# Start-up work moved between queues and engines, one weight step in halves, and idle products in other places: a fused Mamba-2 scan and gated feed-forward kernel

## The chip, the cores and the metric

The kernel runs on one core of a Trainium2 chip. The time is device microseconds (us) of one execution. The kernel before took 350.05, 351.15 and 351.86 us in three runs; the median is 351.15 us. The profile is of a further execution, which took 353.19 us and whose span, from the first to the last instruction, is 351.4 us.

Engines are named as the profile names them. PE is the matrix engine TensorE, and PEld its weight loads; DVE is VectorE, ACT is ScalarE, POOL is GpSimd, and SP is the engine whose queue issues most DMAs. A "q" after a name (SPq, ACTq) means that the engine's sequencer issues a DMA or waits.

## The reference

Inputs are x (4, 8, 768, 32), a (4, 8, 768), B and C (4, 8, 768, 16), and the weights w_in (256 x 2048) and w_out (2048 x 256). The weights are double precision in DRAM. The computation, cut to what matters:

```python
# per batch and head, in chunks of 32 steps
cum = np.cumsum(np.log(np.clip(a, 1e-6, 1.0)), axis=-1)      # within a chunk
L = np.exp(cum[..., :, None] - cum[..., None, :]) * causal   # decay from step j to step i
y = ((C @ B.T) * L) @ x + (C @ state) * np.exp(cum)
state = np.exp(cum[..., -1:]) * state + sum_j(B_j x_j * np.exp(cum[..., -1:] - cum_j))
# then tokens x 256 -> 2048 -> 256
X = y.transpose(0, 2, 1, 3).reshape(3072, 256)
h = X @ w_in
out = (h / (1 + np.exp(-1.702 * h))) @ w_out
```

## The kernel before, in words

**Tokens and groups.** The 3072 tokens form six groups of 512. A group is two pairs of 128-token chunks, and the scan works on chunks of 64 tokens. For each group the scan gives `yT`, 256 features by 512 tokens. `hidden(g, f)` multiplies it by block f of `w_in` (16 blocks of 128 hidden features, two products of 512 columns each, line 881) and applies the gate on ACT (line 885). `project_all` multiplies the gated blocks by `w_out` (line 979). Group 0, and the first four blocks of group 1, go this plain way. The rest uses a scheme with seven products in place of eight (lines 937, 947, 1042 and 1049), fed with sums and differences of weight blocks that DVE makes (`mix_in`, `mix_w`).

**Weights.** They arrive as 64-bit words and are made into 32-bit floats on the chip, in ten pieces (`PIECES`). The first four pieces are two blocks of `w_in` each, pieces 4 and 5 four blocks each, and the last four pieces are `w_out`. For each piece, `fetch` issues two DMAs from SP; `fields` (lines 192 and 195) takes exponent and mantissa bits on DVE; `clamp` (lines 203 and 204) forms the power of two on ACT; `rounded` (line 208) adds the low word on DVE; `join` (lines 219 and 225) sets the sign and multiplies on DVE. `narrow(i)` runs `rounded(i)`, `fields(i + 1)` and `join(i)` in this order. Piece 4 is blocks eight to eleven. All of it runs next to the products of group 0, which wait for `w_in` block by block.

**The start.** The first four chunks are worked in log space. `az0` (rows of a) comes in by four small DMAs, two on SP and two on ACT. DVE clips it (line 338), ACT takes the logarithm (line 340), and a DVE scan gives `cum` (line 342). PE writes a causal mask (line 545) and then the differences of `cum` (`differ`, line 551) into PSUM; ACT exponentiates them into L (line 572). `load_first` brings C by four DMAs from ACT and B by four from SP, and DVE transposes both (line 612). POOL multiplies the transposed C by a head mask (`mask_first`, line 645). PE then forms the scores (line 677), the state increments (line 708) and the outputs (lines 825 and 813). DVE applies L to the scores in `weigh` (line 688). Directly behind `weigh(0)` stands `fetch(1, held=True)`, whose one-element `memset` on DVE (line 171) holds SP until then; pieces 1 to 5 and the rest of a are issued behind it on SP.

**Selectors.** POOL builds small 0/1 tables by `memset` and `affine_select`: `pick0`, the identity, the causal mask `below`, `same` (a 128 x 256 table of which one column in 32 is read), `pick`, and `whose` (64 x 384), in this order and ahead of `mask_first`. `whose` is used by products at lines 509 and 498, `pick` on ACT at line 363.

**Idle products.** `keep_busy(5, 0)` runs five products of ones with 192 columns at the start (line 437), `pads(n, t)` is n products of 32 x 32, and `dense(2)` is two more of 256 columns (line 1153). Their results are not used. In `hidden` for group 1, some of the products are cut into two or four by columns, by a count in lines 876 to 878: the first three into four and the next five into two.

**The order.** Each engine runs its instructions in the order in which they are written; `in_order` at the end pins this. A wait on one engine holds everything behind it on the same engine. A single-precision product stands in the profile as two MATMUL and two LDWEIGHTS records. DMAs of SP and ACT share eight semaphores in turn, so a DMA also waits for the landing of the one eight before it.

Of the kernel before, what the change touches and what calls it, by code (L numbers as in the profile page):

```python
# [8 lines left out]
FP32 = mybir.dt.float32  # L9
# [3 lines left out]
ALU = mybir.AluOpType  # L13
AX = mybir.AxisListType

GELU_SCALE = 1.702
P = 128
# [18 lines left out]
def kernel(  # L36
# [31 lines left out]
    nc = tc.nc  # L68
# [4 lines left out]
    NB, NH, S, D = x.shape  # L73
    N = B.shape[-1]
    BH = NB * NH
    DM, DF = moe_w_in.shape[0], moe_w_in.shape[1] // 2
# [3 lines left out]
    NK = DM // P  # L80
# [4 lines left out]
    PG = CG // 2  # L85
    R = 4
    Q = NH // R
# [7 lines left out]
    const = ctx.enter_context(tc.tile_pool(name="const", bufs=1))  # L95
    raw = ctx.enter_context(tc.tile_pool(name="raw", bufs=3))
    wide = ctx.enter_context(tc.tile_pool(name="wide", bufs=2))
    ssd = ctx.enter_context(tc.tile_pool(name="ssd", bufs=2))
# [11 lines left out]
    w_in = const.tile([P, NF, NK, P], FP32, name="w_in")  # L110
    w_out = const.tile([P, 2, NF, P], FP32, name="w_out")
# [17 lines left out]
    def load_first(name, queues):  # L129

        src = {"B": B, "C": C}[name]
        t = blocks[name, 0] = raw.tile([P, 2, PG * P], FP32, tag="z", name=f"z{name}0", bufs=2)
        for r in range(R):
            queues[r].dma_start(
                out=t[32 * r:32 * r + 32],
                in_=src[0, Q * r:Q * r + Q, :TG].rearrange("q (i f) n -> i q (f n)", i=32))
# [21 lines left out]
    bits, pieces = {}, {}  # L158
# [27 lines left out]
    mantissa, power = {}, {}  # L186
# [11 lines left out]
    def clamp(i):  # L198


        e = power[i]
        z = e.bitcast(FP32)
        nc.scalar.activation(z, e, AF.Relu, scale=-8.0, bias=edge[:, 0:1])
        nc.scalar.activation(e, z, AF.Relu, scale=-1.0, bias=edge[:, 1:2])

    def rounded(i):

        nc.vector.scalar_tensor_tensor(out=mantissa[i].bitcast(FP32), in0=bits[i][0],
                                       scalar=2.0 ** -32, in1=mantissa[i],
                                       op0=ALU.mult, op1=ALU.add)  # L210
# [1 line left out]

    NEXT = {1: (6,), 5: (9,)}

    def join(i):

        name, f, n = PIECES[i]
        hi, m, p2 = bits.pop(i)[1], mantissa.pop(i), power.pop(i)
        nc.vector.scalar_tensor_tensor(out=p2, in0=hi, scalar=0x80000000, in1=p2,
                                       op0=ALU.bitwise_and, op1=ALU.bitwise_or)  # L220
        if name == "in":
            dst, h = w_in[:, f:f + n].rearrange("p f k e -> p (f k e)").unsqueeze(1), 1
        else:
            dst, h = w_out[:, :, f:f + n].rearrange("p c f e -> p c (f e)"), 2
        nc.vector.scalar_tensor_tensor(  # L225
            out=dst, in0=m.bitcast(FP32).rearrange("p (h e) -> p h e", h=h),
            scalar=2.0 ** -20, in1=p2.bitcast(FP32).rearrange("p (h e) -> p h e", h=h),
            op0=ALU.mult, op1=ALU.mult)
        for n in NEXT.get(i, ()):
            fetch(n)  # L230

    def narrow(i):
        rounded(i)
        if i + 1 < len(PIECES):
            fields(i + 1)
        join(i)


    scratch = dram.tile([NC, 2, NB * NH, H], FP32, name="scratch")
# [33 lines left out]
    for r in range(R):  # L273
        (nc.sync, nc.scalar)[r % 2].dma_start(
            out=az0[32 * r:32 * r + 32].rearrange("p k s -> p (k s)"),
            in_=a[:2, :, :TG].rearrange("b h (c s) -> (b h) c s", c=PG))
# [3 lines left out]
    def table(f):  # L280

        nc.scalar.activation(early, early, f)

    table(AF.Ln)
    load_first("C", [nc.scalar] * R)
    load_first("B", [nc.sync] * R)
    fetch(0)
    load(0, "x")
# [9 lines left out]
    def picker(name, n, head, group):  # L298
        t = const.tile([P, n, Q], FP32, name=name)
        nc.gpsimd.memset(t, 1.0)  # L300
        for r in range(R):
            rows = t[32 * r:32 * r + 32]
            nc.gpsimd.affine_select(out=rows, in_=rows, pattern=[[-group, n], [-head, Q]],
                                    compare_op=ALU.is_equal, fill=0.0, base=-head * Q * r,
                                    channel_multiplier=1)
        return t
# [3 lines left out]
    ident = const.tile([P, P], FP32, name="ident")  # L310
# [6 lines left out]
    for side in SIDES:  # L317
        nc.gpsimd.affine_select(out=below[side], in_=below[side], pattern=[[1, H]],
                                compare_op=ALU.is_ge, fill=-1e5, base=0,
                                channel_multiplier=-1)  # L320
# [9 lines left out]
    def fold_ident(k, engine=nc.vector):  # L330
# [6 lines left out]
    fold_ident(0)  # L337
    nc.vector.tensor_scalar(out=az0, in0=az0, scalar1=1e-6, scalar2=1.0, op0=ALU.max,
                            op1=ALU.min)
    nc.scalar.activation(cum, az0, AF.Ln)  # L340
    table(AF.Exp)
    nc.vector.tensor_tensor_scan(
        out=cum.rearrange("p k s -> p (k s)"), data0=carry.rearrange("p k s -> p (k s)"),
# [13 lines left out]
    def pick_a(p):  # L357
# [5 lines left out]
            nc.scalar.activation(X[:, :, q], az[:, c:c + 2], AF.Copy, scale=pick[:, b, q:q + 1])  # L363


    same = ssd.tile([P, NH, D], FP32, tag="BT", name="same")
    nc.gpsimd.memset(same, 1.0)
    nc.gpsimd.affine_select(
        out=same, in_=same, pattern=[[-N, NH], [0, D]], compare_op=ALU.is_ge,
        fill=0.0, base=0, channel_multiplier=1)  # L370
    nc.gpsimd.affine_select(
        out=same, in_=same, pattern=[[N, NH], [0, D]], compare_op=ALU.is_ge,
        fill=0.0, base=N - 1, channel_multiplier=-1)
    pick = picker("pick", NB, 1, NH)
    whose = const.tile([32 * PG, 1 + PG, NH, N], FP32, name="whose")
    nc.gpsimd.memset(whose, 1.0)
    for i, n, head in ((0, 1, PG), (1, 2, PG), (0, 0, 1)):
        t = whose[32 * i:32 * i + 32, n:n + 1]
        nc.gpsimd.affine_select(out=t, in_=t, pattern=[[-1, 1], [-head, NH], [0, N]],
                                compare_op=ALU.is_equal, fill=0.0, base=-max(n - 1, 0),  # L380
                                channel_multiplier=1)

    part = const.tile([P, Q], FP32, name="part")
    nc.vector.tensor_reduce(
        out=part, in_=same[:, :, 0].rearrange("p (r q) -> p q r", q=Q), op=ALU.add, axis=AX.X)


    Ls, BE, st = {}, {}, {}
# [33 lines left out]
    def pads(n, t):  # L425

        for i in range(n):
            c = 32 * (i % R)
            nc.tensor.matmul(out=t[c:c + 32, :32], lhsT=ones[:32, :32], rhs=ones[:32, :32],
                             start=True, stop=True, tile_position=(0, c), skip_group_check=True)  # L430

    def keep_busy(n, m):

        t = busy
        pads(m, t)
        for i in range(n):
            nc.tensor.matmul(out=t[:, :3 * H], lhsT=ones,
                             rhs=ones[:, :H].unsqueeze(1).to_broadcast([P, 3, H]),
                             start=True, stop=True, skip_group_check=True)
# [138 lines left out]
    def bank(name):  # L578
        return ps.tile([P, 4 * P], FP32, tag="ff", name=name)

    def area(name):
        return psa.tile([P, R, 4 * P], FP32, tag="cb", name=name)
# [73 lines left out]
    def since_start(p, engine=nc.vector):  # L656

        b, c = divmod(2 * p, NC)
        s = st[p]
        tp = s["tp"]  # L660
        s["CsT"] = ssd.tile([P, 2, P], FP32, tag="CsT", name=f"CsT{p}", bufs=3)
        engine.tensor_tensor(out=s["CsT"], in0=tp, in1=since[b][:, c:c + 2], op=ALU.mult)
# [201 lines left out]
    def block(g, j):  # L864
        if g or j < 6:
            gT[g, j] = ffn.tile([P, 2, TG], FP32, tag="gT", name=f"gT{g}_{j}", bufs=6)
        else:
            gT[g, j] = ffn.tile([P, 2, TG], FP32, tag="mg", name=f"gT{g}_{j}", bufs=3)

    def hidden(g, f):  # L870
        j, i = divmod(f, 2)
        if i == 0:
            block(g, j)
        h = bank(f"h{g}_{f}")
        for k in range(NK):
            n = 2 if g == 1 and NK * f + k < 11 else 1
            if n == 2 and NK * f + k < 11 - 8:
                n = 4
            for e in range(n):
                cols = slice(e * TG // n, (e + 1) * TG // n)  # L880
                nc.tensor.matmul(out=h[:, cols], lhsT=w_in[:, f, k], rhs=yT[g][:, k, cols],  # L881
                                 start=(k == 0 and e == 0), stop=(k == NK - 1),
                                 skip_group_check=True)

        nc.scalar.activation(gT[g, j][:, i], h, AF.Silu, scale=GELU_SCALE)
# [262 lines left out]
    busy = bank("busy")  # L1148
# [5 lines left out]
                             rhs=ones[:, :H].unsqueeze(1).to_broadcast([P, 4, H]),  # L1154
                             start=True, stop=True, skip_group_check=True)

    keep_busy(5, 0)
    both = area("ab0")
    for r in range(R):
        mask_banks(0, r, both[:, r])  # L1160
    for r in range(R):
        if r == R - 1:
            pads(0, busy)
        mask_banks(1, r, bank(f"ab1_{r}"))
    turn_first("C")
    turn_first("B")
# [21 lines left out]
    parts_first()  # L1188
    for p in range(PG):
        since_start(p, nc.gpsimd)  # L1190
    clamp(0)
    keep_first()
    dense(2)
# [7 lines left out]
    fields(2)  # L1201
    clamp(2)
    join(1)
    load(PG)

# [20 lines left out]
    n, p = 2 * PG, 3 * PG  # L1226
# [99 lines left out]
    k = NF // 2 - 1  # L1326
# [6 lines left out]
    for g in range(2, NG):  # L1333
        n, p = (g + 1) * PG, (g + 2) * PG
# [14 lines left out]
        def mask_third(k):  # L1349
# [4 lines left out]
            C=lambda: combine(g - 1), t=turn_third, b=start_third, u=lambda: mask_third(n),  # L1354
# [39 lines left out]
        k = NF // 2 - 1  # L1394
# [42 lines left out]
```

## Time and profile before

| what | before |
|---|---|
| median of three runs | 351.15 us (350.05 to 351.86) |
| the profiled execution: its time, its span | 353.19 us, 351.4 us |
| PE busy | 342.7 us, 98% |
| DVE busy | 254.2 us, 72% |
| ACT busy | 153.2 us, 44% |
| POOL busy | 13.2 us, 4% |
| read from DRAM, written | 22.15 MB, 3.24 MB |

The busy share of an engine is an average over the whole span. PE is busy nearly all the time, so the time is the sum of its work and its few gaps. DVE is at nine tenths or more of many slices in the first quarter, where the weights are converted. Idle time of an engine other than PE costs something only where PE ends up waiting for it.

### The profile page before, as it was taken

How to read it: one execution, taken by the hardware profiler on the slowest of the kernel's cores; microseconds unless marked ns; L12 is line 12 of the kernel's file. 1: busy time of each engine (PE TensorE's matmuls, PEld its weight loads, DVE VectorE, ACT ScalarE, POOL GpSimd, SP SyncE). 2: the span in 40 equal slices, each digit the busy share in tenths (PEclk: the TensorE clock that was granted, in tenths of full speed). 3: DMA queues.
4: the chain of work that ended last, by engine and by line, in shares of the span. 5: the costliest groups of instructions: out<-in, count | busy, mean ns of one | idle time of the engine just before them, and what ended most of it. 6: DMA issues, size and time to landing. Idle time of an engine off the chain costs nothing.

```text
span 351.4 us, 8124 instructions
## 1 busy us (share of the span) xinstructions
PE 342.7 (98%) x3386; PEld 273.7 (78%) x3386; DVE 254.2 (72%) x473; ACT 153.2 (44%) x350; POOL 13.2 (4%) x41
## 2 busy tenths in 40 slices
PE   8998999998999999999999999999999999999996
PEld 6633444546888888888888888888888888889996
DVE  5989997999678999658997457788464554455463
ACT  5788584104553422644432544432554331553320
POOL 8300000100000100000000000000000000000000
PEclk9999999999999999999999999999999999999999
DMA  6598889563525300426504026400000300000301
GB/s 157 133 321 194 215 185 221 93 94 72 104 49 120 76 0 2 75 62 135 101 19 65 0 58 127 76 0 2 1 4 3 53 9 0 0 2 0 62 0 60
DMA packets 89979, 25.91 MB, mean 74 GB/s; under 512 B 73432, under 2 KB 87128, under 8 KB 89944
## 3 DMA queue, kind: packets, MB, share of 16 engines
q1 hardware_dynamic: 89112, 24.88, 33.4%
q10 hardware_dynamic: 832, 0.52, 0.5%
q8 instruction: 26, 0.43, 0.5%
q14 instruction: 9, 0.07, 0.1%
HBM read 22.15 MB, written 3.24 MB: 72 GB/s over the span
## 4 chain that ended last, share of the span: by engine, by line
PE 88%; DVE 5%; DMA 4%; SPq 1%; issue 1%; ACT 0%; DVEq 0%
PE acc L1042 28%; PE X L937 18%; PE Y L947 14%; PE o L979 8%; PE acc L1049 7%; PE h L881 6%; DMA bits<-in_moe_w_in_dram 3%; PE y L825 2%; PE cb L677 2%; PE y L813 1%; PE A L708 1%; SPq L180 1%; DVE p L192 1%; DVE w_in L225 1%; DMA az<-in_a_dram 1%
## 5 line engine op out<-in xcount | busy, mean ns | idle before, releaser
L942 ACT ACTIVATE ac<-X 128x256 f32<-128x256 f32 x76 | 29.0, 382 | 78.7 <-PE X L937 78.3
L1042 PE MATMUL acc<-mg,mw 128*128 128x256 f32 x192 | 54.5, 379 | 0.0
L914 ACT ACTIVATE gT<-gT 128x512 f32<-128x512 f32 (+1 forms) x76 | 39.3, 519 | 33.4 <-DVE gT L1069 32.9
L1069 DVE TENSOR_TENSOR gT<-Y,ac 128x512 f32<-128x512 f32 x38 | 26.2, 688 | 36.8 <-PE Y L947 28.7
L937 PE MATMUL X<-my,mi 128*128 128x256 f32 x152 | 45.1, 379 | 0.0
L1069 DVE TENSOR_TENSOR gT<-Y,b 128x256 f32<-128x256 f32 x38 | 15.8, 418 | 34.8 <-PE Y L947 34.8
L1042 PEld LDWEIGHTS acc<-mg,mw 128*128 128x128 f32 x192 | 36.5, 190 | 5.0
L881 PE MATMUL h<-yT,w_in 128*128 128x512 f32 (+2 forms) x108 | 35.9, 486 | 1.8 <-DVE w_in L225 1.8
L1042 PE MATMUL acc<-gT,w_out 128*128 128x256 f32 x128 | 35.5, 379 | 0.0
L881 PEld LDWEIGHTS h<-yT,w_in 128*128 128x128 f32 x108 | 18.2, 190 | 18.0 <-issue 12.4
L937 PEld LDWEIGHTS X<-my,mi 128*128 128x128 f32 x152 | 28.1, 190 | 3.7
L979 PE MATMUL o<-gT,w_out 128*128 128x512 f32 x64 | 28.6, 597 | 0.0
L905 DVE TENSOR_TENSOR mg<-gT 128x512 f32<-128x512 f32 x40 | 27.2, 680 | 0.0
L1042 PEld LDWEIGHTS acc<-gT,w_out 128*128 128x128 f32 x128 | 24.2, 190 | 3.4 <-ACT yT L852 0.2
L942 ACT ACTIVATE b<-X 128x256 f32<-128x256 f32 x38 | 14.6, 383 | 20.5 <-PE X L937 20.1
L937 PE MATMUL X<-yT,w_in 128*128 128x256 f32 x76 | 23.2, 389 | 0.0
L947 PE MATMUL Y<-my,mi 128*128 128x256 f32 x76 | 22.7, 381 | 0.1
L947 PE MATMUL Y<-yT,w_in 128*128 128x256 f32 x76 | 22.7, 381 | 0.0
L947 PE MATMUL Y<-yT,mi 128*128 128x256 f32 x76 | 22.6, 381 | 0.0
L937 PE MATMUL X<-my,w_in 128*128 128x256 f32 x76 | 22.5, 379 | 0.0
L979 PEld LDWEIGHTS o<-gT,w_out 128*128 128x128 f32 x64 | 11.8, 190 | 13.2 <-issue 12.7
L399 DVE TENSOR_TENSOR_SCAN L<-a,idents 128x1024 f32<-128x1024 f32 x9 | 20.5, 2277 | 0.1
(153 smaller groups left out, 545.8 us busy)
## 6 DMA issues: line engine op xcount, KB each, us to landing
a<-scratch SPq DMA_DIRECT2D x18, 256.0 KB, 4.9
bits<-in_moe_w_out_dram SPq DMA_DIRECT2D x8, 512.0 KB, 5.8
x<-in_x_dram SPq DMA_DIRECT2D x24, 128.0 KB, 3.0
out_dram<-ob SPq DMA_DIRECT2D x40, 64.0 KB, 1.9
bits<-in_moe_w_in_dram SPq DMA_DIRECT2D x8, 256.0 KB, 4.5
bits<-in_moe_w_in_dram SPq DMA_DIRECT2D x4, 512.0 KB, 10.9
b<-in_B_dram SPq DMA_DIRECT2D x20, 64.0 KB, 2.8
af<-in_a_dram SPq DMA_DIRECT2D x3, 384.0 KB
```

The costliest lines, as they stand in the source:

```text
L399: nc.vector.tensor_tensor_scan(out=L, data0=ra[p].rearrange("p k e -> p (k e)"), data1=idents.rearrange("p h i -> p (h i)"), initial=0.0, ...
L677: nc.tensor.matmul(out=s["cb"][side, r, k].rearrange("p (q i) -> p q i", q=Q), lhsT=BT[rows, k, side], rhs=CT[rows, k, :, side], start=Tru ...
L881: nc.tensor.matmul(out=h[:, cols], lhsT=w_in[:, f, k], rhs=yT[g][:, k, cols], start=(k == 0 and e == 0), stop=(k == NK - 1), skip_group_ch ...
L905: nc.vector.tensor_tensor(out=t[:, 0:2], in0=B[:, :, 1], in1=B[:, 0], op=ALU.subtract)
L914: nc.scalar.activation(o, i, AF.Silu, scale=GELU_SCALE)
L937: nc.tensor.matmul(out=s["X"], lhsT=lhsT, rhs=rhs, start=i == "1", stop=i == "4", skip_group_check=True)
L942: nc.scalar.activation(copy, s["X"], AF.Copy)
L947: nc.tensor.matmul(out=o, lhsT=lhsT, rhs=rhs, start=s.pop("new", False), stop=i != "5", skip_group_check=True)
L979: nc.tensor.matmul(out=o[c], lhsT=w_out[:, c, f], rhs=gT[g, f // 2][:, f % 2], start=(f == 0), stop=(f == NF - 1), skip_group_check=True)
L1042: nc.tensor.matmul(out=acc[g][0][i][:, cols], lhsT=w, rhs=h[:, cols], start=(j == 0 and k == 0 and (i, 0) in begins), stop=(j == NF // 2 - ...
L1049: nc.tensor.matmul(out=o[k] if type(o) is list else o[:, cols], lhsT=h[:, cols], rhs=w, start=(j == 0 and (i, k) in begins), stop=(j == NF ...
L1069: nc.vector.tensor_tensor(out=o, in0=v, in1=w, op=ALU.add)
```

## The change

Eight edits, none of which alters what is computed:

1. `join` can work in parts; piece 4 (blocks eight to eleven) is joined in two halves of two blocks. Each half is one instruction of line 219 and one of line 225 at half the width.
2. C's four first DMAs go alternately to SP and ACT instead of all to ACT; on SP they stand ahead of B's.
3. `whose` is no longer built by POOL: three ACT copies out of the identity fill it, ahead of the logarithm on ACT.
4. `same` shrinks from 128 x 256 to 128 x 8.
5. POOL builds `pick` after the two `since_start` products (line 662) instead of ahead of `mask_first`.
6. `keep_busy(5, 0)` becomes `keep_busy(2, 0)`, followed by `pads(15, busy)`.
7. In `hidden` for group 1, only the first two products are cut, each into two.
8. An empty `pads(0, busy)` is dropped.

On PE this is three products fewer and fifteen more at the start, and twelve fewer in the first four blocks of group 1, so its program is as long as before.

```diff
-    def join(i):
+    def join(i, parts=1):
         name, f, n = PIECES[i]
+        n //= parts
+        low, m, p2 = bits.pop(i)[1], mantissa.pop(i), power.pop(i)
+        for k in range(parts):
+            cols, fs = slice(k * n * DM, (k + 1) * n * DM), slice(f + k * n, f + (k + 1) * n)
+            nc.vector.scalar_tensor_tensor(out=p2[:, cols], in0=low[:, cols], scalar=0x80000000,
+                                           in1=p2[:, cols], op0=ALU.bitwise_and, op1=ALU.bitwise_or)
...
+            nc.vector.scalar_tensor_tensor(
+                out=dst, in0=m[:, cols].bitcast(FP32).rearrange("p (h e) -> p h e", h=h),
+                scalar=2.0 ** -20, in1=p2[:, cols].bitcast(FP32).rearrange("p (h e) -> p h e", h=h),
+                op0=ALU.mult, op1=ALU.mult)
...
-        join(i)
+        join(i, 2 if i == 4 else 1)
...
-    load_first("C", [nc.scalar] * R)
+    load_first("C", [nc.sync, nc.scalar] * PG)
     load_first("B", [nc.sync] * R)
...
+    whose = const.tile([32 * PG, 1 + PG, NH, N], FP32, name="whose")
+    for i, n, head in ((0, 1, PG), (1, 2, PG), (0, 0, 1)):
+        e = 32 * i + max(n - 1, 0)
+        nc.scalar.copy(whose[32 * i:32 * i + 32, n],
+                       ident[32 * i:32 * i + 32, e:e + head * NH:head].unsqueeze(2).to_broadcast(
+                           [32, NH, N]))
     nc.scalar.activation(cum, az0, AF.Ln)
...
-    same = ssd.tile([P, NH, D], FP32, tag="BT", name="same")
+    same = const.tile([P, NH], FP32, name="same")
...
-    pick = picker("pick", NB, 1, NH)
-    whose = const.tile([32 * PG, 1 + PG, NH, N], FP32, name="whose")
-    nc.gpsimd.memset(whose, 1.0)
-    for i, n, head in ((0, 1, PG), (1, 2, PG), (0, 0, 1)):
-        t = whose[32 * i:32 * i + 32, n:n + 1]
-        nc.gpsimd.affine_select(out=t, in_=t, pattern=[[-1, 1], [-head, NH], [0, N]],
-                                compare_op=ALU.is_equal, fill=0.0, base=-max(n - 1, 0),
-                                channel_multiplier=1)
...
-            n = 2 if g == 1 and NK * f + k < 11 else 1
-            if n == 2 and NK * f + k < 11 - 8:
+            n = 2 if g == 1 and NK * f + k < 2 else 1
+            if n == 2 and NK * f + k < 2 - 8:
                 n = 4
...
-    keep_busy(5, 0)
+    keep_busy(2, 0)
+    pads(15, busy)
...
-        if r == R - 1:
-            pads(0, busy)
...
     for p in range(PG):
         since_start(p, nc.gpsimd)
+    pick = picker("pick", NB, 1, NH)
     clamp(0)
```

More of the change, by code (lines that the diff above doesn't have):

```diff
@@ L213 @@
     NEXT = {1: (6,), 5: (9,)}
-    def join(i):
+    def join(i, parts=1):
         name, f, n = PIECES[i]
[L218 to L228, printed above, removed]
+        n //= parts
[4 more added lines that the diff above has]
+                                           in1=p2[:, cols], op0=ALU.bitwise_and, op1=ALU.bitwise_or)
+            if name == "in":
+                dst, h = w_in[:, fs].rearrange("p f k e -> p (f k e)").unsqueeze(1), 1
+            else:
+                dst, h = w_out[:, :, fs].rearrange("p c f e -> p c (f e)"), 2
+            nc.vector.scalar_tensor_tensor(
+                out=dst, in0=m[:, cols].bitcast(FP32).rearrange("p (h e) -> p h e", h=h),
+                scalar=2.0 ** -20, in1=p2[:, cols].bitcast(FP32).rearrange("p (h e) -> p h e", h=h),
+                op0=ALU.mult, op1=ALU.mult)
         for n in NEXT.get(i, ()):
@@ L363, in pick_a @@
             nc.scalar.activation(X[:, :, q], az[:, c:c + 2], AF.Copy, scale=pick[:, b, q:q + 1])
-    same = ssd.tile([P, NH, D], FP32, tag="BT", name="same")
+    same = const.tile([P, NH], FP32, name="same")
     nc.gpsimd.memset(same, 1.0)
     nc.gpsimd.affine_select(
-        out=same, in_=same, pattern=[[-N, NH], [0, D]], compare_op=ALU.is_ge,
+        out=same, in_=same, pattern=[[-N, NH]], compare_op=ALU.is_ge,
         fill=0.0, base=0, channel_multiplier=1)
     nc.gpsimd.affine_select(
-        out=same, in_=same, pattern=[[N, NH], [0, D]], compare_op=ALU.is_ge,
+        out=same, in_=same, pattern=[[N, NH]], compare_op=ALU.is_ge,
         fill=0.0, base=N - 1, channel_multiplier=-1)
-    pick = picker("pick", NB, 1, NH)
-    whose = const.tile([32 * PG, 1 + PG, NH, N], FP32, name="whose")
-    nc.gpsimd.memset(whose, 1.0)
-    for i, n, head in ((0, 1, PG), (1, 2, PG), (0, 0, 1)):
-        t = whose[32 * i:32 * i + 32, n:n + 1]
-        nc.gpsimd.affine_select(out=t, in_=t, pattern=[[-1, 1], [-head, NH], [0, N]],
-                                compare_op=ALU.is_equal, fill=0.0, base=-max(n - 1, 0),
-                                channel_multiplier=1)
     part = const.tile([P, Q], FP32, name="part")
     nc.vector.tensor_reduce(
-        out=part, in_=same[:, :, 0].rearrange("p (r q) -> p q r", q=Q), op=ALU.add, axis=AX.X)
+        out=part, in_=same.rearrange("p (r q) -> p q r", q=Q), op=ALU.add, axis=AX.X)
     Ls, BE, st = {}, {}, {}
```

## The prediction

> **What bounds the kernel now.** I read the page's busy shares, then PE's waits, then the chain that ended last, then the timeline of the places these named.
>
> ```profile
> PE 342.7 (98%) x3386; PEld 273.7 (78%) x3386; DVE 254.2 (72%) x473; ACT 153.2 (44%) x350; POOL 13.2 (4%) x41
> ```
>
> PE is idle for 351.4 - 342.7 = 8.7 us in all, so the whole question is which of these microseconds go. PE's waits:
>
> ```profile
> PE h L881 <- DVE w_in L225: 1.8, 2, 1.0
> PE y L825 <- issue: 1.5, 1, 1.5
> ...
> PE b L624 <- ACT L L572: 0.5, 1, 0.5
> ```
>
> From 17.6 us on PE works without a gap except for three: 0.85 and 0.98 us for `w_in` blocks (at 22.1 and 33.65 us), and 1.49 us at 80.3 us for nothing that a semaphore shows. The second, on DVE and on PE:
>
> ```profile
> 30.98 1.26 DVE L219 SCALAR_TENSOR_TENSOR p<-bits,p 128x1024 uint32<-128x1024 uint32 x1
> 32.28 1.22 DVE L225 SCALAR_TENSOR_TENSOR w_in<-m,p 128x1024 f32<-128x1024 f32 x1
> ```
> ```profile
> 33.65 3.67 PE L881 MATMUL h<-yT,w_in 128*128 128x512 f32 x8 [0.98 <-DVE w_in L225]
> ```
>
> This is `join(4)`: PE had run out of blocks at 32.67 and waits for all four. Before it the chain goes over DVE and DMA:
>
> ```profile
> 8.89 0.93 DVE p L192
> ...
> 11.82 1.17 DVE L L688 x2
> ...
> 15.88 7.23 DMA bits<-in_moe_w_in_dram
> ```
>
> The big weight DMAs are held by a `memset` on DVE behind `weigh(0)` (line 688); that stands behind `fields(0)`, which waited for the first weights and then ran three times its usual 0.44 us:
>
> ```profile
> 7.91 2.03 POOL L645 TENSOR_TENSOR CT<-Ct,part 128x512 f32<-128x512 f32 x2
> ```
> ```profile
> 8.89 1.33 DVE L192 TENSOR_SCALAR p<-bits 128x512 uint32<-128x512 uint32 x1 [0.65 <-DMA bits<-in_moe_w_in_dram]
> 10.14 0.42 DVE L195 TENSOR_SCALAR m<-bits 128x512 uint32<-128x512 uint32 x1
> ```
>
> The third gap, in the chain:
>
> ```profile
> 79.26 1.03 PE y L825 x68
> 80.30 1.49 issue
> 81.78 0.65 PE y L825 x36
> ```
>
> [...] line 192 took 1.33 us while POOL's line 645 ran to 9.94, and 0.44 us elsewhere. [...] the trace has one such packet at 79.35 to 80.28 us and PE idle until 81.78, 1.5 us after it landed. [...] the idle products start every 0.32 us from 1.21 us; from 4.6 us on the next products come every 0.11 us.
>
> **The change part by part.**
>
> *Halves of piece 4.* Line 219 starts at 30.98. A 512-wide one takes 0.69 us (rows at 15.69 and 20.58), the 512-wide line 225 also 0.69. First half: 30.98 + 0.69 + 0.04 + 0.69 = 32.40; with the 0.13 us that PE needed after 33.50 it can start at 32.53, before it has finished the block ahead (32.67). The gap of 0.98 goes. The price: two more instructions, and the second half ends at about 33.72, 0.22 later. PE needs block ten only at about 36, so that is covered; behind it DVE is full until 52, so block thirteen meets the `since` scan that frees its PSUM bank (line 540, over at 42.71 + 0.22; PE would come at 43.83 - 0.98 = 42.85). I take 0.15 off. Gain 0.8 (from 0.5 to 0.98).
>
> *PE's instruction blocks.* Twelve products more at the front are 48 records, and they are taken off again in group 1 from 84 us on. So between the start and 84 us each block border falls 48 instructions earlier in the program. Counted from the program, the border of the stall lies 176 instructions into the 256 of the burst at 79.26. [...] But the DMA engines were full with the `a<-scratch` rows (issued at 73.80 and 74.43; DMA share 0.9 to 1.0 from 74 to 79), and the packet started only at 79.35. [...] The stall of 1.49 us goes. [...]
>
> But DVE caps this gain. From 64.5 to 86 it is full (scans, `mix_in`, transposes), and `gain` at 87.89 on PE needs its last result of 85.99. PE would come 0.8 + 1.49 earlier, its first half (0.4 us) needs only the older result, so 0.2 is lost.
>
> *Fewer cuts in group 1.* 28 records took 3.54 and 16 took 3.65 us, against 8 x 0.4375 = 3.50 each for uncut ones (24 in 10.5 us at 38.68). Gain 0.15.
>
> *The start.* POOL: `same` goes from 1.23 us (three rows) to about 0.5, estimated from the 0.2 us of the selects of 32 x 8; `pick` (1.55) and `whose` (1.52) leave. So `mask_first` waits only for the transposed C. C's last DMA landed at 6.23; on two queues it is issued 0.5 earlier, at about 3.25 (it waits for az0's landing), and lands at 5.7 to 5.9. The transpose starts when the scan and line 387 are over, about 5.95 instead of 6.31, and line 645 runs from 7.0 to 9.05 instead of 7.91 to 9.94. The clip at line 338 no longer shares its time with a POOL select: 0.52 becomes about 0.27 (a third of line 350's 768 elements plus a fixed part), so logarithm, scan and line 551 come 0.25 earlier. The `whose` copies: [...] inside ACT's wait (until 4.82 now, about 4.55 then). [...] `pick` is built by about 14.7 and first used at 34.4.
>
> Against this, two C DMAs (about 0.5 us each) go ahead of B, the weights and x on SP; B's fewer waits give back some 0.25. The first weights are issued at 5.3 and 5.8 instead of 4.51 and 4.98, and land at about 9.45 (bounds 9.1 and 9.9) instead of 8.79. `fields(0)` is then clear of POOL: 9.5 to 10.25 instead of 8.89 to 10.56. `weigh(0)` starts at about 11.45 instead of 11.74 and the weight DMAs follow: gain 0.25, from 0.6 gained to 0.2 lost. x lands some 0.6 later (12.9); lines 708, 825 and 813 and the first two blocks move with it, and that is paid out of the 0.85 us gap before 22.1. Queued behind them: `clamp(1)` on ACT, with about 0.2 us to spare.
>
> *Idle products.* Two products end at 2.49. The fifteen small ones are 30 records. No row shows them alone: moving 64 columns at half clock is 0.053 us by the rate above (384 columns in 0.32), twice that if loads and products alternate, so they end between 4.1 and 5.7. Line 551 is due at about 5.75, with eight mask products (0.9 us warm, 1.7 cold) between. I take nothing, at worst 1.5 us of PE's start, most of it under DVE's wait for the weights.
>
> Sum: 0.8 + 1.49 - 0.2 + 0.15 + 0.25 = 2.5. Against the profiled execution 353.19 - 2.5 = 350.7 (span 348.9); it lies 2.04 above the median of the runs, from which 351.15 - 2.5 = 348.7. A measurement can tell about 0.5% from no change, here 1.8 us.
>
> **The rivals.**
>
> *The stall stays or moves* (0.17). For: [...] a new border may starve another burst. Against: the free DMA time from 71 to 74. Then 0.8 + 0.15 + 0.25 = 1.2 are left: 350.0.
>
> *The start gives the gain back* (0.15). Weights at 9.9 or later, x past the 0.85 us gap: 0.8 lost there, or DVE's full stretch keeps `w_in` late. Then 2.5 - 0.25 - 0.9: 349.8.
>
> *PE stays at half clock* (0.08). [...] PE has 10.74 us of work between 6.0 and 17.6, which would take twice as long. 0.85 is absorbed by the gap; the `w_in` wait (0.98) is gone in any case. Then 351.15 + 10.7 - 0.85 - 0.98 - 1.49 - 0.15 = 358. It decides from about 3.5 us of extra cold work on, which is half clock until line 551 and the first scores are done. [...]
>
> **How the numbers follow.** The likeliest case has 0.58 (own range 348.0 to 349.3); 0.02 is left for what I don't see. Faster by over 0.5% means below 349.4: nearly all of the likeliest and a few of the start's, 0.58. Within: 0.31. Slower: the cold clock and a few mishaps, 0.11. The range from 347.9 (all bounds good: 0.6 at the start, the whole 0.98) to 351.3 leaves out the cold case and what is beyond the other bounds.
>
> **What would show it.** PE's waits: one wait for line 225 left, under 0.9 us; no issue wait near 79 us; PE on block eight at about 32.3. Line 192's first row at 0.4 us; POOL's line 642 from 7.0; the held fetch at about 12.75; line 548 (was 551) starting before 6.0 and as short as now (0.70 and 0.73 us a batch). `gain` waiting for DVE at about 86 shows the cap. Wrong if the idle products last past 5 us, if weights land after 9.9, or if PE then waits where it didn't.

## The result, and the profile after

The kernel after took 353.56 us (median of 15 runs, 352.12 to 356.4), the kernel before on the same chip 350.71 us (15 runs, 349.94 to 352.94). The ratio is 1.008, with a 95% interval of 1.006 to 1.010: 0.8% slower, where 0.7% faster had been forecast.

The two profiled executions hide this. Their spans are 351.4 us before and 351.6 us after, because the profiled execution of before was itself a long one (353.19 us against a median of 350.71), while that of after lies at its median. So the kernel before was profiled again, unchanged (the first experiment below): 350.81 us, with a span of 349.0. That is the execution to compare with. PE's waits, of the kernel after and then of that second profile of the kernel before (engine, line, releaser: us in total, times, longest):

```profile
PE h L878 <- DVE w_in L228: 2.2, 1, 2.2
PE busy L434 <- DVE ones L299: 1.2, 1, 1.2
PE ab L548 <- DVE part L384: 0.5, 1, 0.5
PE b L621 <- ACT L L569: 0.5, 1, 0.5
PE X L934 <- ACT ac L939: 0.3, 1, 0.3
```
```profile
PE busy L437 <- DVE ones L296: 1.2, 1, 1.2
PE h L881 <- DVE w_in L225: 0.6, 2, 0.3
PE b L624 <- ACT L L572: 0.5, 1, 0.5
PE y L825 <- issue: 0.3, 1, 0.3
```

(From the middle of the file on, lines of the kernel after are three lower: 878 is 881 before.) Both waits that the prediction wanted to remove, 0.98 us for piece 4 and 1.49 us of issue at line 825, are gone after. But in the second profile of before they are all but gone as well: 0.31 us is left of the first and nothing of the second. In exchange PE's wait for the second piece of `w_in` (block two) has grown from 0.33 to 2.22 us. The timeline of PE in the kernel after, start and duration:

```profile
1.21 1.65 PE L434 MATMUL busy<-ones 128*128 128x192 f32 x4 [1.21 <-DVE ones L299]
2.79 0.65 PE L426 MATMUL busy<-ones 32*32 32x32 f32 x30
3.37 1.89 PE L542 MATMUL ab<-below,identb 128*128 128x256 bf16 x8
5.80 1.16 PE L548 MATMUL ab<-cum,pick 32*64 32x128 f32 x32 [0.55 <-DVE part L384]
6.89 1.24 PE L548 MATMUL ab<-minus,cum 32*128 32x128 f32 x16
...
25.14 13.97 PE L878 MATMUL h<-yT,w_in 128*128 128x512 f32 x32 [2.22 <-DVE w_in L228]
```

The large differences (line 548) ran at half speed: 1.16 and 1.24 us a batch, where the first profile of before had 0.70 and 0.73. The last line is as foreseen in one respect: blocks two to nine, 32 records, run without a break through the place where piece 4 had been waited for. The chain of the kernel after shows what came late ahead of them:

```profile
14.74 0.37 SPq L180
...
16.19 6.62 DMA bits<-in_moe_w_in_dram
...
22.90 0.43 DVE p L192
```

The same places in the second profile of before, on the chain and on PE:

```profile
13.58 0.37 SPq L180
...
19.84 0.43 DVE p L192
```
```profile
22.08 10.54 PE L881 MATMUL h<-yT,w_in 128*128 128x512 f32 x24 [0.33 <-DVE w_in L225]
32.92 3.67 PE L881 MATMUL h<-yT,w_in 128*128 128x512 f32 x8 [0.31 <-DVE w_in L225]
```

Against the second profile of before, block two starts 25.14 - 22.08 = 3.06 us later. Of this, 14.74 - 13.58 = 1.16 are the later held fetch, and 1.90 are the transfer: piece 2 (counted from 0), behind whose `fields` the second piece is joined, has landed 8.07 us after the held fetch (22.81) instead of 6.17 (19.75). Part of this belongs to one execution: in all the other profiles it took 6.0 to 7.6 us. At the first product of `acc` 103.32 - 100.83 = 2.5 us are left, and from there to the end both take 248.2 to 248.3 us. So everything is decided in the first 103 us, and the questions are why the fetch is late and, above all, why the weights come more slowly.

### The profile page after: what moved, and what is told of

It is laid out like the page before. It is cut to its first block, busy times and chain, and to the rows that moved or that the text cites. A ratio compares the mean times of both kernels' runs of the same rounds, so it can differ in the third digit from the quotient of the medians.

```text
span 351.6 us, 8127 instructions
## 1 busy us (share of the span) xinstructions
PE 343.4 (98%) x3386; PEld 271.1 (77%) x3386; DVE 253.0 (72%) x475; ACT 154.0 (44%) x353; POOL 10.8 (3%) x37
## 4 chain that ended last, share of the span: by engine, by line
PE 93%; DMA 3%; DVE 2%; SPq 1%; ACT 1%; issue 0%; DVEq 0%
PE acc L1039 28%; PE X L934 18%; PE Y L944 14%; PE h L878 9%; PE o L976 8%; PE acc L1046 7%; PE y L822 2%; PE cb L674 2%; DMA bits<-in_moe_w_in_dram 2%; PE y L810 1%; PE ab L548 1%; PE A L705 1%; DMA az<-in_a_dram 1%; DVE c L1070 0%; SPq L180 0%
## 5 line engine op out<-in xcount | busy, mean ns | idle before, releaser
L878 PE MATMUL h<-yT,w_in 128*128 128x512 f32 (+1 forms) x84 | 35.5, 576 | 2.2 <-DVE w_in L228 2.2
L878 PEld LDWEIGHTS h<-yT,w_in 128*128 128x128 f32 x84 | 15.6, 190 | 19.8 <-issue 17.6
L976 PEld LDWEIGHTS o<-gT,w_out 128*128 128x128 f32 x64 | 11.8, 190 | 13.2 <-issue 12.4
```

What stands on the lines that cost most here:

```text
L976: nc.tensor.matmul(out=o[c], lhsT=w_out[:, c, f], rhs=gT[g, f // 2][:, f % 2], start=(f == 0), stop=(f == NF - 1), skip_group_check=True)
```

## The experiments

H stands below for the halves of piece 4, C for the order of the C rows, W for the selectors (`whose`, `same`, `pick`), P for the idle products with the fewer cuts. Ratios are to the kernel before, run in between on the same chip, where its median stayed at 351.16 to 351.40 us. No experiment leaves out anything of the computation; idle products have no readers.

**The kernel before again** (no edit).

> The kernel before, unchanged, for a second profile. If the 1.49 us gap of PE in line 825 near 80 us belongs to the program (the block border and the full DMA queues), it stands here again and the span is near 351.4. If it depends on the execution, it is gone or elsewhere and the span is near 349.0 (median 350.71 less the 1.8 that lie outside the span). PE's clock: [...] line 551's first batch takes between 0.70 and 1.16 us from run to run; if the five wide products fix it, it is 0.70 again.

350.81 us, span 349.0; its waits are shown above. PE's stall of 1.49 us near 80 us and two thirds of the waits for `w_in` belonged to one execution. Line 551's first batch took 0.86 us, between the two values.

**First theory: PE's clock.** As the differences ran at half speed, the first suspect was P.

```diff
-    keep_busy(2, 0)
-    pads(15, busy)
+    keep_busy(5, 0)
+    pads(12, busy)
```


> The changed kernel with five wide idle products and twelve small ones in place of two and fifteen: the number of PE instructions is the same at every place behind them. Clock theory ([...] PE stays at half clock until 10.4 us): line 548's batches fall from 1.16 and 1.24 to 0.70 and 0.73 us, the held fetch from 14.7 to 13.0, and the time to about 349.7, ratio to the kernel before 0.995 to 0.999. Queue theory (C ahead of B makes the first weights land at 9.76 instead of 8.79, and that holds everything): batches may get shorter, but the fetch stays at 14 or later and the time above 352.

352.69 us, 1.0062 (1.0027 to 1.0097). The differences ran at full speed (0.69 and 0.73 us a batch) and most of the loss was still there.

P alone on the kernel before (two large and fifteen small products, the fewer cuts):

> The kernel before with the idle products and the cuts of the changed one alone (two wide and fifteen small, two cuts). Clock theory: line 551's batches 1.16 and 1.24 us, the held fetch about 1.7 later, and the time about 353.0 to 354.0, ratio 1.006 to 1.010. Queue theory: no slower than the kernel before, ratio 0.996 to 1.001. Instruction-block theory (the shift by 48 starves a burst): a wait of PE for nothing that a semaphore shows, of 1 us or more, before 84 us.

351.66 us, 1.0014 (0.9993 to 1.0035), though the profiled execution stayed at half speed until about 18 us.

The kernel after with P undone:

> The changed kernel with the idle products and the cuts of the kernel before (five wide, eleven cuts); halves, C on two queues, selectors by ACT and the shorter POOL set-up stay. Clock theory: batches 0.70 and 0.73 us, held fetch near 13.0, PE on block eight without a wait, time 349.5 to 350.2, ratio 0.996 to 0.999. Queue theory: ratio 1.004 or more, with the first weights at 9.8 and the fetch at 14 or later. Should the block border at line 825 matter, it stalls here as in the profile of before.

352.76 us, 1.0036 (1.0004 to 1.0067). With the products of before about half of the loss stays, within a wide interval. P can't be all of it.

**Second theory: the order of SP's queue, and each part alone.** C puts two issues ahead of B, the weights and x.

```diff
-    load_first("C", [nc.scalar] * R)
+    load_first("C", [nc.sync, nc.scalar] * PG)
```


> The kernel before with one line of the change: the four C rows are issued in turn by SP and ACT, ahead of B; everything else as before. Queue theory (two more issues of about 0.5 us ahead of B, the first weights and x on SP put the weight stream and with it DVE's conversions late until about 88 us): first weights land near 9.6 instead of 8.8 us, the last w_out piece lands at 58 us or later instead of 55 to 57, Be ends near 87.5 instead of 84 to 86, time 1.004 to 1.006 of before. Clock theory (the idle products and when PE gets its full clock): the products are those of before, so 1.000 within 0.002. Halves theory (DVE holds PE after the shorter wait): 1.000 too.

351.65 us, 1.0011 (0.9997 to 1.0025). The first weights landed at 9.39 us, as late as the theory said, but the last `w_out` piece was taken up at 54.87 us, as early as in the kernel before. Piece 4 in halves alone (`join(i, 2 if i == 4 else 1)`):

> The kernel before with one part of the change: piece 4 of w_in is converted by halves; PE's program, the queues and the selectors are as before. The prediction's step: the wait of 0.98 us at 33.65 goes and 0.8 is gained, 0.9977. Where that wait is only 0.3 us in most executions, as in the second profile of the kernel before: 0.999 to 1.000. Queue theory: 0.999 to 1.000, no harm. Halves theory (the second half comes 0.22 us later on DVE, which is full behind it, and all later pieces with it): 1.001 to 1.003, with DVE work near 50 us and the Be end 0.2 us or more later.

350.89 us, 0.9994 (0.9977 to 1.001): no measurable gain, and no harm. W alone:

> The kernel before with one part of the change: the selectors copied by ACT, the narrow tile of GpSimd, the pick tile built later; the C rows, products and halves as before. The prediction's step: mask_first earlier, the fields clear of GpSimd, the clip 0.2 us shorter, so weigh(0) and the held fetch 0.3 to 0.6 us earlier: 0.998 to 1.000. Queue theory: 0.999 to 1.000. Selector theory (three copies on ACT of 0.9 us in all come ahead of the logarithm[...]): 1.002 to 1.004, with a later logarithm or a wait of DVE near 15 us.

353.85 us, 1.0051 (1.0025 to 1.0077). This is the part that costs most. But not in the way that the selector theory said: the scan starts at 5.49 us, only 0.23 later than in the second profile of before, and what follows makes up for it. The weights are fetched at 13.24 us, earlier than there (13.58), and yet the last piece of `w_in` lands at 31.93 instead of 28.97 us (in a long execution: 355.3 us of 350.43 to 355.55). The kernel after with C undone:

> The kernel after with one line undone: the four C rows are all on ACT again, so B, the first weights and x go out on SP as early as before; products, halves and selectors stay as in the change. Queue theory: the first weights land near 8.8 us, the last w_out piece lands at 55 to 57 us, time 1.000 to 1.003 of before against 1.008 for the whole change. Clock theory (late full clock): 1.006 to 1.008, as the whole change. If the parts only add up in pieces of equal size, about 1.005.

352.79 us, 1.0049 (1.0028 to 1.007). The weights went out early, the last `w_out` piece was taken up only at 57.88 us: as the main cause the queue theory falls, too.

**Third theory: addresses.** What do the kernels with W have in common? The view of the DMA queues (queue, kind: packets, MB, share of 16 engines) of the second profile of before, and of the kernel after:

```profile
q1 hardware_dynamic: 89112, 24.88, 33.9%
```
```profile
q1 hardware_dynamic: 89272, 25.02, 34.7%
```

The packets are as good as the same in number and size, but take longer. Adding up the time of all packets in the traces and dividing by the 16 engines gives 119.4 to 122.4 us in the profiles without W so far and 125.1 to 127.2 in those with it (127.4 in that of the kernel with P undone, an execution of 356.29 us).

What W does to a DMA is in the allocation: `same` moved from a work pool into the pool `const`, which grew by 32 bytes per partition, and every tile of the pools behind it moved along. `bits` of the first piece starts at byte 79,104 of its partitions before (309 x 256), and at 79,136 after. The landing tiles of x, B, C and a lie 32 bytes further as well, and so does `ob`, from which most of the output leaves. All of them started on a border of 256 bytes and now start 32 bytes past one. That this costs time was the author's guess; no run so far shows it by itself. The test moves addresses and nothing else:

```diff
-    part = const.tile([P, Q], FP32, name="part")
+    part = const.tile([P, Q + 8], FP32, name="part")[:, :Q]
```


> The kernel before with one const tile (part) 32 bytes wider per partition, of which nothing uses the added bytes: same instructions, same queues, but every tile of the pools allocated behind const (the landing tiles of x, B, C, the weights, a, and the work tiles) lies 32 bytes further, so that they start 32 bytes past a 256-byte border instead of on one. Address theory (the selectors part costs its 0.5% because its narrow same tile added 32 bytes to const, and DMA writes to such addresses take longer): time 1.004 to 1.006 of before, the DMA queue's share near 34.9% instead of 33.5 to 34, its packets about 126 to 127 us per engine in sum instead of 119 to 122. Selector theory (the copies on ACT, GpSimd's or pick's new place): 1.000, packets as before.

353.66 us, 1.0053 (1.0025 to 1.008). 32 bytes that nobody uses cost as much as W. In the profiles the two kernels run alike, each starting its fetch at 13.58 us, until the weights come. Of the shifted kernel the queue, the issues of the larger `w_in` pieces (times, KB each, median us from issue to landing), PE's wait, and the chain:

```profile
q1 hardware_dynamic: 89112, 24.88, 35.3%
...
bits<-in_moe_w_in_dram SPq DMA_DIRECT2D x4, 512.0 KB, 10.5
```
```profile
PE h L881 <- DVE w_in L225: 2.0, 2, 1.1
```
```profile
19.57 11.07 DMA bits<-in_moe_w_in_dram
```

Unshifted, the same issue line reads 9.7:

```profile
bits<-in_moe_w_in_dram SPq DMA_DIRECT2D x4, 512.0 KB, 9.7
```

The last piece of `w_in` landed at 30.64 instead of 28.97 us, 1.67 later, PE waited 2.0 instead of 0.6 us for `w_in`, and the span is 1.6 us longer. The engines' own instructions did not change: DVE's durations add up to 274.1 and 273.9 us, ACT's to 169.1 and 169.3, PE's records to 1013.8 and 1013.6. What differs are the packets. Where PE waited rests on this one pair, and such waits vary: the first profile of before, on borders too, waited 1.8 us for `w_in`, and its last piece landed at 29.65 us. That the shift costs time is shown by the medians. Shifts by 64, 256 and 128 bytes (`Q + 16`, `Q + 64`, `Q + 32`):

> As the shift by 32 bytes, but by 64. If what counts is a border of 64 bytes, 1.000 and 119 to 122 us of packets per engine; if it is one of 256 bytes [...], about as slow as the shift by 32: 1.004 to 1.006 and 126 us or more. Selector theory: 1.000.

> The kernel before with the same const tile wider by 256 bytes instead of 32 or 64: all tiles behind it move, but stay on 256-byte borders. Address theory: 1.000 within 0.0015, packets 119 to 122.6 us per engine. If moving the tiles by any amount costs: 1.005.

> The same with 128 bytes. If only borders of 256 bytes count: 1.004 to 1.006 and 125 us of packets per engine or more; if a border of 128 is enough: 1.000 and at most 122.6.

| shift | ratio, 95% interval | x packet, mean ns | output packet, mean ns | 1,024-byte packet, mean ns | packets per engine, us |
|---|---|---|---|---|---|
| 0 (second profile of before) | 1 | 13.0 | 11.8 | 53.1 | 122.4 |
| 32 | 1.0053 (1.0025 to 1.008) | 13.4 | 12.8 | 54.3 | 127.7 |
| 64 | 1.0049 (1.0029 to 1.0068) | 13.2 | 13.1 | 53.8 | 125.0 |
| 128 | 1.0019 (1.0001 to 1.0037) | 13.0 | 11.8 | 53.6 | 122.8 |
| 256 | 1.0004 (0.9985 to 1.0024) | 13.0 | 11.8 | 53.0 | 119.8 |

(The means are over all packets of a kind in each trace. Of the 45,056 packets of 128 bytes, 24,576 bring x into SBUF and 20,480 take output rows out of `ob`, from about 94 us on; the order of the issues tells them apart. The 9,088 of 1,024 bytes are mostly weights.)

32 and 64 bytes cost, 256 do not; 128 lie between, where neither of the two expectations was met, and the interval overlaps those of both sides.

The output packets separate cleanly: 11.7 to 11.9 ns on borders of 256 bytes and at the shift by 128, 12.8 to 13.1 in all other profiles. That fits the border of 256: pieces of 128 bytes at 32 or 64 bytes past it cross every second one, at 128 none. These packets are read from SBUF, and they are not what costs the time. From the first product of `acc`, at 100 to 106 us, to the end every profile takes 247.7 to 248.5 us, shifted or not (with one exception of 249.1, on borders). The loss comes before, and there most packets are written into SBUF.

Of these the x packets cross the borders just as often, and yet took 13.0 to 13.2 ns on average, on and off them alike, but for the first 4,096: 13.0 to 13.1 on borders and at the shift by 128, 14.1 to 14.8 at 32 and 64 bytes past, in all but one profile (13.1 in the kernel after). The 1,024-byte packets took 51.4 to 54.2 ns on borders and 53.9 to 56.0 at 32 bytes past; the ranges overlap a little. The last piece of `w_in` landed 14.7 to 16.8 us after the held fetch on borders and 16.8 to 19.3 at 32 bytes past, but 15.5 in the one profile at 64 and 16.3 at 128. So the address is shown to cost the time, and before the first product of `acc`; which transfers pay, and by what mechanism, is not.

**The change without the shift.** `same` is made 256 bytes wide per partition, of which 32 are used, so that everything behind it is back on a border:

```diff
-    same = const.tile([P, NH], FP32, name="same")
+    same = const.tile([P, 8 * NH], FP32, name="same")[:, :NH]
```


> The whole change, with its same tile 256 bytes wide per partition instead of 32 (only the first 32 are used), so that all tiles behind const are back on borders of 256 bytes. Address theory: the 0.5% go, 1.001 to 1.004 of before (C order and products left, each about 0.001), packets 119 to 122 us per engine. Selector theory: 1.008 as the whole change.

352.46 us, 1.003 (1.0011 to 1.0049). The queue is back below the level of before:

```profile
q1 hardware_dynamic: 89272, 25.02, 33.0%
```

And H and W alone, on borders:

> Halves of piece 4 and the selectors part, with the same tile 256 bytes wide; C order and products as in the kernel before. Address theory: the selectors part is harmless once it moves no addresses, 0.997 to 1.000 of before. Selector theory: 1.004 to 1.005.

350.64 us, 0.9979 (0.9965 to 0.9994): **faster than both kernels**, by a little. To it C, and then P in place of C, were added:

> Halves, selectors and the C order of the change, on 256-byte borders; the idle products of the kernel before. Halves and selectors alone gave 0.9979. If the C order is what is left (first weights and x 0.9 us later): 1.001 to 1.003. If the products are: 0.998 to 0.999.

> Halves, selectors and the idle products of the change, on 256-byte borders; the C order of the kernel before. If the products are what is left (full clock late in some executions, held fetch at 13 to 16.5 us): 1.001 to 1.003. If the C order is: 0.998 to 0.999.

C: 1.0007 (0.999 to 1.0024). P: 1.0037 (1.0015 to 1.0058). Both are slower than H and W alone; for C the intervals still overlap a little. In the profiled execution with P, PE stayed at half speed until about 18 us; with the five large products it was at full speed by 6.2. The timelines of PE, first with P, then without:

```profile
3.36 1.89 PE L542 MATMUL ab<-below,identb 128*128 128x256 bf16 x8
6.25 1.16 PE L548 MATMUL ab<-cum,pick 32*64 32x128 f32 x32 [1.00 <-DVE part L384]
...
11.29 1.12 PE L621 MATMUL b<-ident,Bt 128*128 128x128 f32 x4 [0.46 <-ACT L L569]
```
```profile
4.57 1.55 PE L542 MATMUL ab<-below,identb 128*128 128x256 bf16 x8
6.24 0.69 PE L548 MATMUL ab<-cum,pick 32*64 32x128 f32 x32
...
9.33 0.66 PE L621 MATMUL b<-ident,Bt 128*128 128x128 f32 x4 [0.46 <-ACT L L569]
```

The held fetch goes out at 17.11 against 13.24 us, and the span is 353.2 against 349.6. But this is not what every execution with P does. The two that were profiled with W, P and even borders are the longest or next to the longest of their 22 runs (355.00 of 350.38 to 355.00; 355.16 of 350.35 to 355.21), while the shortest runs are as short as without P. In the pair shown a late clock costs about 3.5 us; that it comes in a part of the executions only is concluded from the times. Is it the size of the small products, or that PE runs out of work at 5.25 us? A third large product, and then none of the small ones:

```diff
-    keep_busy(2, 0)
+    keep_busy(3, 0)
     pads(15, busy)
```


> Halves, selectors and the idle products of the change on 256-byte borders, with three large products in place of two ahead of the fifteen small ones: the mask products then end at about 5.95 instead of 5.25 us. If what matters is that PE has work until about 5.7: full clock by 6.5 us in the profile, 0.997 to 1.000. [...] half clock until 10 us or later in the profile, 1.002 to 1.005.

352.15 us, 1.001 (0.9989 to 1.0031); but the profiled execution, the longest of its 14 at 355.14 us, was at half speed until about 18 us although the mask products lasted until 5.89. Two large products and no small ones:

> The same with two large products and no small ones: PE's mask products end at about 4.7 us. If the end of the work matters: half clock to 10 us or later, 1.003 to 1.006, as with the small ones or slower. If the small products were a hindrance: faster than with them, 1.000 or less.

353.32 us, 1.0053 (1.0035 to 1.0071), all six runs between 352.80 and 354.17; half speed until about 11 us, and 2.3 us of issue stalls in this execution. With the third large product the ratio was lower, though the intervals overlap, so a late clock may come less often with more work early. But it still came with work until 5.89 us, and it did not come in the profile of the kernel with C undone, where the same two large and fifteen small products stood ahead of the same masks and the differences ran at 0.69 and 0.73 us a batch.

Each trace also records when PE's clock rose to full. From the rise to the fall after the last product it stayed up for 98, 100, 101 or 102 times 3.413 us, in every profile: it changes on a grid of such steps, whose position differs from execution to execution. With five large products it rose at 4.2 to 7.2 us in all 13 profiles, a spread of less than one step. With two large and fifteen small ones it rose at 4.69 (C undone), 10.56 (the change), 17.75, 17.93 and 18.22, with three and fifteen at 17.99, and with the two alone at 10.71. So with fewer large products it can come up to four steps later. What decides at which step it rises was not settled.

**All together.** Five parts (H, W, C, P and the shift by 32), taken as additive and fitted to the twelve ratios of kernels made of just these parts, each weighted by its interval, come to -0.09, -0.02, +0.14, +0.27 and +0.45%, with uncertainties of 0.05 to 0.09. Their sum is 0.75%, against 0.8 measured. One of the twelve misses the fit by 0.21% (H, W and P on even borders: 0.37 where the fit has 0.16), the others by up to 0.13, so the parts are not strictly additive.

## Why the prediction was wrong, point by point

**The missing term.** The prediction costed `same` as POOL's time alone. That the tile also changed its pool, and what the pool's size does to every address behind it, is in no step of it, and this is the largest term: +0.45% by the fit, about 1.6 us, shown by the shift alone (1.0053) and by its removal (1.003 in place of 1.008). The instructions, the queues and their order, which the prediction compared, don't show it.

**PE's instruction blocks.** The step "The stall of 1.49 us goes" was worth 60% of the sum, and it fell. In twelve executions with the same PE program the stall near 80 us was 1.49, 0, 0, 0.42, 0, 0.27, 0.85 and 0 us (before twice, C, H, and the shifts by 32, 64, 256 and 128; gaps above 0.1) and 0.81, 0.83, 0 and 0 (W, P undone, and H and W on even borders without and with C): 0.39 on average. In six with the 48 records moved ahead (P, the change, the change with five large products, C undone, and the two with P on even borders) it was 0, 0, 0, 0.61, 0.53 and 0.81: 0.33. So on average there was no more than 0.4 us to gain, and no gain from moving the border by 48 instructions shows. When a block of instructions is asked for, no trace shows: that an earlier border would end the stall was the author's estimate, made for a single execution. What its trace has is 26 packets of 16,384 bytes in a queue of kind instruction (`q8`), on average 251 PE records apart; that of 79.35 to 80.28 us is one of them.

**Halves of piece 4.** The mechanism was right: on even borders none of seven profiles with H has a wait there, nor has the change itself; with the shift three still do (0.33, 0.68 and 0.86 us: the change with five large products, C undone, P undone). The size was off. 0.98 us was the wait of the profiled execution; the other four without H and on borders have 0.31, 0.24, 0 and 0.34. H alone measured 0.06% (0.2 us, from 0.8 gained to 0.4 lost), the fit 0.09%, where 0.8 us had been put down.

**Fewer cuts.** 12 records took 3.44 and 8 took 3.63 us, against 3.54 and 3.65 before: 0.12 gained for 0.15 forecast.

**The start.** Side by side its steps came in: line 192's first row at 0.43 us (why it took 1.33 before is not shown, only that POOL's line 645 ran beside it), line 642 on POOL from 6.83 (7.0 forecast), the clip at 0.29 us. The three copies for `whose` took 0.90 us, from 3.57 on, and were over before the logarithm started at 4.61. The first weights landed at 9.76, inside the bounds of 9.1 to 9.9 but 0.3 past the value. With full clock `weigh(0)` started at 11.36 us (H, W and C on even borders; 11.45 forecast), and the held fetch went out at 12.63 (12.75 forecast). Yet C lost 0.14% by the fit. The prediction had paid the later x out of the 0.85 us gap ahead of block two, and that gap is 0.33 us in the second profile.

**Idle products.** The fifteen were over at 3.43 us, below the bounds of 4.1 to 5.7, as 30 records took only 0.65. "I take nothing" failed: this was the rival with a chance of 0.08, PE at half clock, which the trace of the change shows. Its time of 358 was too high by far. It added the whole extra PE work, while the late execution shown lost about 3.5 us, and by the times only a part of the executions is late. One trace can't decide it: the clock changed on steps of 3.413 us whose place differs from execution to execution. With the same five products it rose at 4.66 us in the first profile of before and at 6.85 in the second, and at 4.2 to 7.2 in all 13; with two large and fifteen small ones it rose at 4.69 to 18.22.

**The base.** Above all, the terms were read from an execution that lay 2.0 us above the median and taken off the median. The waits that made this execution long (1.49, and 0.98 instead of 0.31) were the very ones counted as gain: they belonged to the 2.0 us, and most of them could not be gained on the median.

## What to carry to other kernels

Before a wait of one execution is counted as a gain, compare that execution with the median: what it has more than the others is likely its own. When an edit adds, widens or moves a tile, compare the start addresses of all tiles behind it, not only the instructions; here 32 bytes cost more than all the other parts of the change could win, and with the tile padded to 256 bytes, halves and selectors without the rest of the change left a small gain. Idle products that are to raise a clock are judged over many executions, as a profile shows one.

## What the runs showed of the hardware that was not expected

- Landing and output tiles that start 32 or 64 bytes past a border of 256 bytes made the kernel 0.5% slower, 256 bytes did not. In sum the packets took 125 to 128 us per engine in place of 119 to 123.
- Packets of 128 bytes that leave SBUF from such places took 12.8 to 13.1 ns in place of 11.7 to 11.9, and 11.8 at a shift of 128 bytes. Those of the same size that are written into SBUF, but for the first 4,096, took 13.0 to 13.2 ns on average everywhere. Packets of 64 bytes hardly changed (10.7 to 10.9 ns).
- 30 records of idle 32 x 32 products took 0.65 us at half clock, 0.02 us each.
- PE's clock stayed at full for a whole number of steps of 3.413 us (98, 100, 101 or 102) in each of the 20 profiles, and the time at which it rose differed between executions with the same first products: from 4.69 to 18.22 us with two large and fifteen small ones.
- A PE stall near 80 us that no semaphore shows, at one place of one program, was between 0 and 1.49 us in twelve executions.
